# A Fourier mix and a dense block on one core: partial sums of the early dense products put off, and a spare PSUM bank for their refills

## The chip, the cores and the metric

The kernel runs on one core of a Trainium2 chip. A core has a matrix engine (TensorE, PE in the profile, with PEld for its weight loads), a vector engine (VectorE, DVE), a scalar engine (ScalarE, ACT), GpSimd (POOL) and a sync engine (SP) that here only issues loads. Each engine works off its own queue in order; 16 DMA engines move the data that SP and POOL ask for. Matmuls write into PSUM, which this kernel uses as eight banks of 128 x 512 float32; a bank is read and written by VectorE and ScalarE too. The metric is the device time of one execution in microseconds (us), the median of several runs.

## The reference

x has 2048 tokens of width 640. The output mixes a two-dimensional Fourier transform with a dense block, by a gate per token:

```python
g = sigmoid((x * gate_w).sum(-1, keepdims=True))
a = einsum("bsd,ed->bse", x, dft_hid_re); b = einsum("bsd,ed->bse", x, dft_hid_im)
y = einsum("ts,bse->bte", dft_seq_re, a) - einsum("ts,bse->bte", dft_seq_im, b)
h = einsum("bsd,df->bsf", x, w1) + b1          # 640 -> 1728
act = h * tanh(softplus(h))                    # Mish
out = g * y + (1 - g) * einsum("bsf,fd->bsd", act, w2)
```

All is float32. The kernel computes the transposed output, 640 rows by 2048 tokens.

## The kernel before, in words

**Products.** A float32 operand is split in two float32r tiles, a high part (ScalarE, L344 or L335) and a low part (VectorE, L345 or L336), and a product of two blocks takes three matmuls, all at L350 (mm3: high x high, high x low, low x high). Large products are done with Winograd's form of Strassen's scheme: sums and differences of blocks (tt, L314) save an eighth of the block products, and partial products are copied out of PSUM and back into it (copy, L323: f<-ps is a copy out to SBUF, called to_sbuf; ps<-f is a refill of a bank, onto which the next matmuls add).

**Stages.** First, the sequence transform x with cosines and sines, four problems (q = 0 to 3), each with a first, a second and a third part over 8 pairs of row blocks. The first parts of the problems come at the start of the kernel: 1, then 2, 3 and 0. They have only nine matmuls a step (three banks: two in self.a, one in self.d1), and between their steps stand the steps of the early dense products. Then the second and third parts of all four problems (some 118 to 445 us), the hidden transform, the rest of the dense product, and the second dense product with the output.

**Early dense products.** They are the top 768 of the 1728 columns of w1 against the first 1024 tokens (two tiles of 512, t = 0 and 1). The depth of 640 is cut in blocks of 128. early_first does the first two pairs of blocks (depth 256), early_second the next two and the fifth block (depth 384). Each has three units (j = 0 to 2), a generator with 7 or 8 steps; a step is one product of 3 or 6 matmuls. A unit works in two banks, a and b. It multiplies b11 into a, copies a out as p, multiplies t1 into b; multiplies b21 onto a and drains a: that is the output for t = 0; copies p back into a (copy(a, p), the refill), multiplies t2 onto it, drains it as u, and so on. Four outputs of a unit of early_first go to DRAM as early. (They are loaded twice: by early_second, and much later by dense_first, as the part that the rest of the dense product starts from.) In early_second the inner function end loads early, adds it to the bank, applies Mish (L624, out_act) and stores the activation as act. So there a drain of a bank is an add on VectorE that also waits for the load of early.

**Order.** Two lines of three units each run side by side with the running product of the sequence transform: line one is units 0 and 2 of early_first and unit 1 of early_second, line two is unit 1 of early_first and units 0 and 2 of early_second. After each of the 24 steps of problems 2, 3 and 0 stands one step of each line. The running product takes three banks and the two units two each, seven of eight. At a turn from one problem to the next (after 8 and 16 steps) three new banks are taken while three old ones are drained.

**Planner.** The program records all operations with their dependences (Graph.add); Graph.run then plays them on a model of the engines and emits each engine's queue in the order that comes out. PE keeps program order. Another engine takes, when it is free, the ready operation with the earliest due time (want) that is granted its buffers. wants() works the due times out backward from PE's order; `by` makes a due time earlier, `since` bars an operation before a time. A buffer pool (psum, FS for 18 tiles of 128 x 512, and others) grants a buffer if more are free than earlier asks are open (granted); an operation that drains PSUM, or follows such a one, is prompt, and one that is not prompt also leaves buffers for prompt ones that are due within 5 us. If nothing can go on, the planner stops with an error ("stuck"). Loads go through SP's queue (L296), stores through POOL's (L306).

Of the kernel before, what the change touches and what calls it, by code (L numbers as in the profile page):

```python
# [27 lines left out]
DELAY, RATE = 2.2, 370e3  # L28
CALM, CALM_DMA, NEAR = 1.0, 3.0, 3.0
GATES = 130.0, 10.0  # L30
GATED = 600.0, 7.0


# [16 lines left out]
class Graph:  # L50
# [75 lines left out]
    def run(self, pools):  # L126

        self.wants()
        for op in self.ops:
            for v in op.vals:  # L130
                if v.pool and (v.ask is None or op.want < v.ask[0]):
                    v.ask = op.want, op.n, id(v)
        for op in self.ops:
            for v in op.vals:
                if v.pool and v.ask[1] == op.n:
                    also = [u.ask[0] for u in op.vals if u.pool is v.pool and u is not v]
                    if also:
                        v.ask = min(v.ask, (max(also), op.n, id(v)))
        for p in pools:
            p.asks = sorted({v.ask for op in self.ops for v in op.vals if v.pool is p})  # L140
            p.soon = sorted({v.ask for op in self.ops if op.prompt for v in op.vals if v.pool is p and v.ask[1] == op.n})
        missing = {op.n: len(op.deps) for op in self.ops}
        free = {e: 0.0 for e in ("PE", "ACT", "DVE", "SP", "POOL")}
        ready = {e: [] for e in free}
        pe = [op.n for op in self.ops if op.engine == "PE"][::-1]
        for op in self.ops:
            if not missing[op.n]:
                insort(ready[op.engine], (op.want, op.n))
        events, now, left, dma = [], 0.0, len(self.ops), 0.0
        waits = sorted({op.since for op in self.ops})  # L150

        def granted(op, blocked):
            for v in op.vals:
                if v.pool and v.t is None:
                    if v.pool in blocked:
                        return False
                    p, n = v.pool, bisect_left(v.pool.asks, v.ask)
                    if not op.prompt:
                        n += bisect_left(p.soon, (v.ask[0] + AHEAD,)) - bisect_left(p.soon, v.ask)
                    if len(p.free) <= n:  # L160
                        blocked.add(v.pool)
                        return False
            return True

        def bequeath(p):
            if p.heir and not p.asks:
                p.heir.free += [p.part(t) for t in p.free]
                p.free = []

        while left:  # L170
            began = False
            for e, line in ready.items():
                if free[e] > now + 1e-9 or not line:
                    continue
                if e == "PE":
                    i = next((i for i, x in enumerate(line) if x[1] == pe[-1]), None)
                    if i is not None and not granted(self.ops[pe[-1]], set()):
                        i = None
                else:
                    blocked = set()  # L180
                    i = next((i for i, x in enumerate(line)
                              if self.ops[x[1]].since <= now and granted(self.ops[x[1]], blocked)), None)
                if i is None:
                    continue
                op = self.ops[line.pop(i)[1]]
                if e == "PE":
                    pe.pop()
                for v in op.vals:
                    if v.pool and v.t is None:
                        v.pool.asks.remove(v.ask)  # L190
                        if v.ask in v.pool.soon:
                            v.pool.soon.remove(v.ask)
                        v.t = v.pool.free.pop(0)
                        bequeath(v.pool)
                op.emit()
                free[e] = now + op.hold
                if e in ("SP", "POOL"):
                    dma = max(now + DELAY, dma) + op.moves
                    end = dma + 0.1
                else:  # L200
                    end = now + op.took + 0.03
                heapq.heappush(events, (end, op.n, False))
                left -= 1
                began = True
            if began:
                continue
            times = [t for e, t in free.items() if t > now + 1e-9 and ready[e]]
            times += [t for t in waits if t > now][:1]
            if events:
                times.append(events[0][0])  # L210
            assert times, ("stuck", left, pe and self.ops[pe[-1]].at, [(p.name, len(p.free)) for p in pools])
            now = max(now, min(times))
            while events and events[0][0] <= now + 1e-9:
                _, n, held = heapq.heappop(events)
                op = self.ops[n]
                if held:
                    insort(ready[op.engine], (op.want, op.n))
                    continue
                for v in op.vals:
                    v.left -= 1  # L220
                    if not v.left and v.pool:
                        p = v.pool
                        p.free.append(v.t)
                        bequeath(p)
                for a in op.after:
                    missing[a.n] -= 1
                    if not missing[a.n]:
                        wait = min(CALM_DMA if op.engine in ("SP", "POOL") else CALM, a.want - now - NEAR)
                        if a.engine in ("ACT", "DVE") and wait > 0:
                            heapq.heappush(events, (now + wait, a.n, True))  # L230
                        else:
                            insort(ready[a.engine], (a.want, a.n))
# [8 lines left out]
def fnet_mish_gate(ctx: ExitStack, tc: tile.TileContext, xn, xt, c_re, c_im, wd_re, wd_im,  # L241
# [56 lines left out]
        op.by, op.since = by, since  # L298
        return v

    def load_of(pool, d, rows=P):
        return load(pool, lambda: d.t, d, rows)

    def store(d, v, rows=P, queue=None):
        queue = queue or STORES
# [313 lines left out]
    def raw(t, k):  # L619
        return load(FS, xt[t, k])  # L620
# [80 lines left out]
        out_act(FC, t, a, a, FR, False)  # L701

    H = FP // 2
    early = {(t, f): dram(f"early{t}_{f}") for t in range(2) for f in range(FP)}

    def w1_twice(k0, fifth=False):

# [37 lines left out]
    def early_first():  # L745
# [3 lines left out]
        def unit(j):  # L749
            a, b = bank(), bank()  # L750
            mm3(a, at["b11", j], x["a11"], True, True)
            p = to_sbuf(a)
            yield
            mm3(b, at["t1", j], x["s1"], True, True)
            yield
            mm3(a, at["b21", j], x["a12"], False, True)
            store(early[0, j], to_sbuf(a))
            copy(a, p)
            yield
            mm3(a, at["t2", j], x["s2"], False, True)  # L760
            u = to_sbuf(a)
            yield
            mm3(a, at["t3", j], x["s3"], False, True)
            v = to_sbuf(a)
            tt(v, b, v, OP.add)
            store(early[1, j + H], v)
            yield
            mm3(b, at["b22", j], x["s4"], False, True)
            tt(u, b, u, OP.add)
            store(early[0, j + H], u)  # L770
            yield
            mm3(a, at["t4", j], x["a22"], False, True)
            store(early[1, j], to_sbuf(a))
            yield
        return [unit(j) for j in range(H)]

    def early_second():
# [4 lines left out]
        def unit(j):  # L782
            a, b = bank(), bank()

            def end(c, t, f):
                o = load_of(FS, early[t, f])
                tt(o, c, o, OP.add)
                out_act(f, t, o, o)
            mm3(a, at["b11", j], x["a11"], True, True)
            p = to_sbuf(a)  # L790
            yield
# [1 line left out]
            yield  # L793
            mm3(a, at["b21", j], x["a12"], False, False)
            mm3(a, at[("d", 0), j], d[0], False, True)
            end(a, 0, j)
            copy(a, p)
            yield
            mm3(a, at["t2", j], x["s2"], False, True)
            u = to_sbuf(a)  # L800
# [9 lines left out]
            yield  # L810
            mm3(a, at["t4", j], x["a22"], False, False)
            mm3(a, at[("d", 0), j], d[1], False, True)
            end(a, 1, j)
            yield
            copy(b, v)
            mm3(b, at[("d", 1), j], d[1], False, True)
            end(b, 1, j + H)
            yield
        kept.update(x, d=d)
        return [unit(j) for j in range(H)]  # L820
# [3 lines left out]
    def early_rests():  # L824
        for t, ks in ((0, ("a11", "a12")), (1, ("a21", "a22"))):
            dense_rest(t, [operand(raw(t, k)) for k in range(2)] + [kept[k] for k in ks] + [kept["d"][t]])

    def dense_first(tp):
        t1, t2 = tp, tp + 2
# [145 lines left out]
    ua, ub = early_first(), early_second()  # L975
    lines = [ua[0], ua[2], ub[1]], [ua[1], ub[0], ub[2]]
    lines = [(u for q in line for u in q) for line in lines]
    for q in (2, 3, 0):
        for _ in sq[q].steps(seq_top):
            for line in lines:  # L980
                next(line, None)
    for line in lines:
        for _ in line:
            pass
# [1 line left out]
    for q in range(4):  # L986
        sq[q].second(seq.low)
        if q == 2:
            gates()
        sq[q].third()  # L990
    hd[0].first(hid.top)
    hd[1].first(hid.top)
    for p in hd:
# [58 lines left out]
```

## Time and profile before

| | |
|---|---|
| median of 3 runs | 865.77 us (864.66 to 866.73) |
| profiled execution, device time | 866.31 us |
| its span, first to last instruction | 864.5 us |
| TensorE busy | 856.1 us (99%), 3754 matmuls |
| VectorE, ScalarE, GpSimd busy | 694.5, 486.9, 91.8 us |
| DMA | 220.27 MB, mean 255 GB/s |
| mean granted TensorE clock | 0.998 |

A row of the timeline reads: start in us, duration, engine, line, operation, output<-inputs by the program's tile names, shapes, count, and in brackets the idle time of the engine before it and what ended it. Matmul durations overlap: matmuls are pipelined, and the time of one is the distance of two starts. A row of waits reads: who waited for whom, us in total, times, longest. A row of windows reads: the stretch, its length, busy time and instructions of PE, PEld, DVE, ACT and POOL, then the granted clock (1.00 is full speed), the mean busy share of the DMA engines, and GB/s. A row of the chain of work that ended last reads: start, us, what.

### The profile page before, as it was taken

To read this page: it belongs to the slowest core of one execution; us is meant where nothing else is said; L and a number is where in the kernel's file an instruction comes from. 1 tells how busy PE (TensorE), PEld (TensorE's weight loads), DVE (VectorE), ACT (ScalarE), POOL (GpSimd) and SP (SyncE) were. 2 spreads that over 40 slices of the span, in tenths; PEclk is the share of its full clock that TensorE was granted. 3 is DMA by queue.
4 is the path that set the end of the run, shared out by engine and by line. 5 is a ranking of instruction groups with operands and counts; after the bars stand their busy time and mean duration, and the time that the engine had idled before them with its cause. 6 is when DMAs were issued, how large, how long until landed. Compare 5 with 4: busy or idle time off the path is not lost.

```text
span 864.5 us, 12193 instructions
## 1 busy us (share of the span) xinstructions
PE 856.1 (99%) x3754; PEld 704.8 (82%) x3754; DVE 694.5 (80%) x1241; ACT 486.9 (56%) x902; POOL 91.8 (11%) x167
## 2 busy tenths in 40 slices
PE   8999999999999999999999999999999999999998
PEld 6887788888888888888888888888888888888886
DVE  7978789986896778677999978997787996758493
ACT  6976776535354654456576733676566764533242
POOL 0122110002000200100020001022222100004000
PEclk9999999999999999999999999999999999999999
DMA  9888786777885957395778839678798876637943
GB/s 331 303 321 303 258 284 235 258 250 268 306 278 177 357 178 233 129 346 194 233 239 314 298 111 368 228 249 304 272 306 314 314 257 239 197 117 170 367 163 122
DMA packets 110946, 220.27 MB, mean 255 GB/s; under 512 B 13920, under 2 KB 18144, under 8 KB 110880
## 3 DMA queue, kind: packets, MB, share of 16 engines
q1 hardware_dynamic: 97184, 177.14, 60.0%
q0 software_dynamic: 13552, 42.22, 13.9%
q8 instruction: 29, 0.48, 0.2%
q14 instruction: 37, 0.30, 0.1%
q10 hardware_dynamic: 144, 0.13, 0.0%
HBM read 174.59 MB, written 44.84 MB: 254 GB/s over the span
## 4 chain that ended last, share of the span: by engine, by line
PE 97%; DMA 2%; DVE 0%; ACT 0%; issue 0%; SPq 0%; ACTq 0%; DVEq 0%
PE ps L350 97%; DMA x<-in_xn_dram 1%; DMA x<-in_w1a_dram 1%; DMA f<-in_c_im_dram 1%; SPq L296 0%; DVE f L314 0%; DVE x L314 0%; DVE r1l L345 0%; DVE r4l L345 0%; ACT r1h L344 0%; ACT ps L323 0%; ACT w19h L335 0%; ACT f L323 0%; DVE f L601 0%; ACT f L599 0%
## 5 line engine op out<-in xcount | busy, mean ns | idle before, releaser
L314 DVE TENSOR_TENSOR f<-f,f 128x512 f32<-128x512 f32 (+1 forms) x322 | 214.2, 683 | 5.1 <-DMA f<-act 2.0
L323 ACT ACTIVATE f<-ps 128x512 f32<-128x512 f32 x149 | 87.1, 595 | 63.4 <-PE ps L350 58.0
L314 DVE TENSOR_TENSOR f<-ps,f 128x512 f32<-128x512 f32 x101 | 66.9, 685 | 44.2 <-PE ps L350 34.2
L306 POOL DMA_DIRECT2D u<-f x40 | 21.6, 541 | 303.2 <-DVE f L314 289.8
L344 ACT ACTIVATE r9h<-f 128x512 fp32r<-128x512 f32 x40 | 25.3, 631 | 29.0 <-PE ps L350 20.5
L306 POOL DMA_DIRECT2D act<-f x52 | 28.1, 541 | 116.8 <-ACT f L624 74.1
L344 ACT ACTIVATE r5h<-f 128x512 fp32r<-128x512 f32 x38 | 24.0, 631 | 28.0 <-PE ps L350 22.2
L314 DVE TENSOR_TENSOR x<-x,x 128x256 f32<-128x256 f32 (+2 forms) x88 | 38.0, 445 | 2.2 <-DMA x<-in_xn_dram 1.5
L344 ACT ACTIVATE r1h<-f 128x512 fp32r<-128x512 f32 x39 | 24.5, 629 | 25.1 <-PE ps L350 19.6
L344 ACT ACTIVATE r4h<-f 128x512 fp32r<-128x512 f32 x38 | 23.9, 630 | 24.3 <-PE ps L350 18.7
L323 ACT ACTIVATE ps<-f 128x512 f32<-128x512 f32 x56 | 33.0, 598 | 8.2 <-DVE f L314 7.8
L344 ACT ACTIVATE r0h<-f 128x512 fp32r<-128x512 f32 x38 | 23.9, 629 | 23.8 <-PE ps L350 14.2
L344 ACT ACTIVATE r6h<-f 128x512 fp32r<-128x512 f32 x38 | 24.0, 631 | 23.2 <-PE ps L350 14.6
L344 ACT ACTIVATE r2h<-f 128x512 fp32r<-128x512 f32 x38 | 23.9, 629 | 22.8 <-PE ps L350 16.6
L344 ACT ACTIVATE r7h<-f 128x512 fp32r<-128x512 f32 x38 | 24.0, 631 | 21.5 <-PE ps L350 11.9
L345 DVE TENSOR_TENSOR r9l<-f,r9h 128x512 fp32r<-128x512 f32 x40 | 27.5, 686 | 10.5 <-ACT r9h L344 10.3
L344 ACT ACTIVATE r3h<-f 128x512 fp32r<-128x512 f32 x39 | 24.5, 628 | 19.9 <-PE ps L350 14.0
L344 ACT ACTIVATE r8h<-f 128x512 fp32r<-128x512 f32 x36 | 22.7, 630 | 21.2 <-PE ps L350 10.9
L345 DVE TENSOR_TENSOR r6l<-f,r6h 128x512 fp32r<-128x512 f32 x38 | 26.1, 686 | 10.4 <-ACT r6h L344 10.2
L345 DVE TENSOR_TENSOR r1l<-f,r1h 128x512 fp32r<-128x512 f32 x39 | 26.7, 686 | 9.0 <-ACT r1h L344 8.6
L624 ACT ACTIVATE f<-f,b1s 128x512 f32<-128x512 f32 x36 | 25.9, 718 | 14.1 <-DVE f L314 13.8
L345 DVE TENSOR_TENSOR r2l<-f,r2h 128x512 fp32r<-128x512 f32 x38 | 26.1, 688 | 9.5 <-ACT r2h L344 8.9
(2185 smaller groups left out, 2696.2 us busy)
## 6 DMA issues: line engine op xcount, KB each, us to landing
f<-in_c_im_dram SPq DMA_DIRECT2D x128, 256.0 KB, 4.7
f<-in_c_re_dram SPq DMA_DIRECT2D x128, 256.0 KB, 4.2
f<-act SPq DMA_DIRECT2D x84, 256.0 KB, 4.6
f<-u SPq DMA_DIRECT2D x80, 256.0 KB, 4.1
act<-f POOLq DMA_DIRECT2D x52, 256.0 KB, 4.0
f<-in_xt_dram SPq DMA_DIRECT2D x42, 256.0 KB, 4.3
u<-f POOLq DMA_DIRECT2D x40, 256.0 KB, 4.2
x<-in_xn_dram SPq DMA_DIRECT2D x24, 320.0 KB, 4.8
```

The costliest lines, as they stand in the source:

```text
L306: dma(queue, lambda: ISSUE[queue].dma_start(d.t, v.t[:rows]), whole(v), whole(d), rows * N * 4)
L314: dve(lambda: nc.vector.tensor_tensor(o.t[rows, x], a.t[rows, y], b.t[rows, z], op=op), whole(a, b), whole(o), n)
L323: act(lambda: nc.scalar.activation(o.t, a.t, AF.Copy, scale=scale), whole(a), whole(o))
L344: act(lambda: nc.scalar.activation(r.t[0][:, :N], src.t[:, :N], AF.Copy), whole(src), [(r, 0)])
L345: dve(lambda: nc.vector.tensor_tensor(r.t[1][:, :N], src.t[:, :N], f32(r.t[0][:, :N]), op=OP.subtract), whole(src) + [(r, 0)], [(r, 1)])
L350: G.add("PE", lambda: nc.tensor.matmul(bank.t, w.t[wn][:, k * P:k * P + P], x.t[xn_][:, :N], start, stop, skip_group_check=True), [(w, (k, ...
L624: act(lambda: nc.scalar.activation(o.t[rows], src.t[rows], AF.Mish, **more), whole(src, table) + whole(b1s) * bias, whole(o), more=0.1)
```

## The change

Four things change:

- early_second no longer adds early. Its function end stores its output tile in DRAM as late; banks a (twice) and b (once) of a unit are drained for it by to_sbuf.
- A new function early_acts, after the third parts of the sequence problems in program order, loads early and late for each of the 12 outputs, adds them in SBUF, applies Mish and stores act. Its loads carry since = 300 + 8 i us (SUMS), its adds are due 8 us later.
- The refill of p goes into a newly taken bank (a = copy(bank(), p)) in place of the bank that was just drained, in both kinds of units. A unit so holds three banks for a while; the eighth is used. copy(b, v) at the end of a unit of early_second stays as it is.
- The second line begins one step behind the first: after the first of the 24 steps only the first line steps. And the planner, where nothing at all can go on, tries once more with a flag (tight) by which a prompt operation counts only prompt asks ahead of it.

```diff
+SUMS = 300.0, 8.0
...
+                    if op.prompt and tight:
+                        n = bisect_left(p.soon, v.ask)
...
+            if not times and not tight:
+                tight = True
+                continue
             assert times, ("stuck", left, pe and self.ops[pe[-1]].at, [(p.name, len(p.free)) for p in pools])
...
-    def load_of(pool, d, rows=P):
-        return load(pool, lambda: d.t, d, rows)
+    def load_of(pool, d, rows=P, since=0.0):
+        return load(pool, lambda: d.t, d, rows, since=since)
...
-    early = {(t, f): dram(f"early{t}_{f}") for t in range(2) for f in range(FP)}
+    early, late = ({(t, f): dram(f"{n}{t}_{f}") for t in range(2) for f in range(FP)} for n in ("early", "late"))
...
             store(early[0, j], to_sbuf(a))
-            copy(a, p)
+            a = copy(bank(), p)
...
-            def end(c, t, f):
-                o = load_of(FS, early[t, f])
-                tt(o, c, o, OP.add)
-                out_act(f, t, o, o)
+            def end(o, t, f):
+                store(late[t, f], o)
...
-            end(a, 0, j)
-            copy(a, p)
+            end(to_sbuf(a), 0, j)
+            a = copy(bank(), p)
...
-            end(a, 1, j)
+            end(to_sbuf(a), 1, j)
             yield
             copy(b, v)
             mm3(b, at[("d", 1), j], d[1], False, True)
-            end(b, 1, j + H)
+            end(to_sbuf(b), 1, j + H)
...
+    def early_acts():
+
+        for i, key in enumerate(early):
+            since = SUMS[0] + SUMS[1] * i
+            o, v = (load_of(FS, d[key], since=since) for d in (early, late))
+            tt(o, o, v, OP.add)
+            G.ops[-1].by = since + SUMS[1]
+            out_act(key[1], key[0], o, o)
...
-    for q in (2, 3, 0):
-        for _ in sq[q].steps(seq_top):
-            for line in lines:
-                next(line, None)
+    for n, _ in enumerate(s for q in (2, 3, 0) for s in sq[q].steps(seq_top)):
+        for line in lines if n else lines[:1]:
+            next(line, None)
...
+    early_acts()
     hd[0].first(hid.top)
```

More of the change, by code (lines that the diff above doesn't have):

```diff
@@ L168, in bequeath @@
                 p.free = []
+        tight = False
         while left:
@@ L205, in run @@
             if began:
+                tight = False
                 continue
```

## The prediction

> **What bounds the kernel now.** I read the page's busy shares first, then what TensorE waited for over the whole run, then the chain of work that ended last, and from there the timelines of the two places where the chain leaves TensorE.
>
> ```profile
> PE 856.1 (99%) x3754; PEld 704.8 (82%) x3754; DVE 694.5 (80%) x1241; ACT 486.9 (56%) x902; POOL 91.8 (11%) x167
> ```
>
> ```profile
> PE ps L350 <- ACT ps L323: 2.4, 2, 1.9
> ```
>
> ```profile
> 7.94 68.75 PE ps L350 x302
> ...
> 92.33 0.59 ACT ps L323
> ...
> 92.96 767.73 PE ps L350 x3377
> ```
>
> TensorE (PE) is the bound, and the diff adds and removes no matmul. So only time in which PE stands still or runs slow can be won. After the start-up there are two such waits in the whole run, both for ScalarE (ACT) writing a PSUM bank (L323, output ps), and the chain leaves PE between 77 and 93 us only. From 92.96 us to 860.69 the chain is PE alone. The next rows are PE's, around both waits and behind them.
>
> ```profile
> 85.12 0.39 PE L350 MATMUL ps<-r0h,w1l 128*128 128x512 f32 x1
> 86.03 0.50 PE L350 MATMUL ps<-r6h,w25h 128*128 128x512 f32 x1 [0.52 <-ACT ps L323]
> ...
> 87.53 0.40 PE L350 MATMUL ps<-w24h,w21h 128*128 128x512 f32 x1
> ...
> 90.72 0.39 PE L350 MATMUL ps<-r1h,w25l 128*128 128x512 f32 x1
> 92.96 0.50 PE L350 MATMUL ps<-r6h,w25h 128*128 128x512 f32 x1 [1.85 <-ACT ps L323]
> ...
> 97.42 0.39 PE L350 MATMUL ps<-r5h,w22h 128*128 128x512 f32 x1
> ...
> 103.78 0.39 PE L350 MATMUL ps<-w24l,w9h 128*128 128x512 f32 x1
> ```
>
> ```profile
> 92.00:94.00 2.00, 1.04 (x4) 0.85 (x5) 1.87 (x4) 2.00 (x4) 0.15 (x1) 0.93 0.80 309
> 94.00:96.00 2.00, 2.00 (x7) 1.52 (x6) 1.93 (x5) 1.15 (x3) 0.39 (x1) 0.50 0.93 346
> ```
>
> At full speed matmuls start (103.78 - 97.42) / 28 = 0.227 us apart. The first wait costs 86.03 - 85.12 - 0.23 = 0.68 us, and the six matmuls behind it 1.50 - 6 x 0.227 = 0.14. The second costs 92.96 - 90.72 - 0.23 = 2.01, and the twelve matmuls from 92.96 to 97.42 take 4.46 where 12 x 0.227 = 2.72 would do: 1.74 more, because the granted clock (the seventh figure of the window rows) fell to 0.50 right behind the wait. Together 4.57 us, 0.53% of the run: the most that the change can win here.
>
> **Why the two refills were late.** Both are the line copy(a, p) of a unit of early_second: bank a, drained after the third product, gets the first product back, and the fourth product adds to it. The ACT and DVE (VectorE) rows before them:
>
> ```profile
> 83.11 0.42 DVE L314 TENSOR_TENSOR x<-x,x 128x256 f32<-128x256 f32 x1 [1.48 <-DMA x<-in_xn_dram]
> ...
> 84.66 0.68 DVE L314 TENSOR_TENSOR f<-ps,f 128x512 f32<-128x512 f32 x1
> ...
> 89.38 0.68 DVE L314 TENSOR_TENSOR f<-ps,f 128x512 f32<-128x512 f32 x1
> ```
>
> ```profile
> 79.20 0.58 ACT L323 ACTIVATE f<-ps 128x512 f32<-128x512 f32 x1
> ...
> 82.01 0.58 ACT L323 ACTIVATE f<-ps 128x512 f32<-128x512 f32 x1
> ...
> 85.38 0.60 ACT L323 ACTIVATE ps<-f 128x512 f32<-128x512 f32 x1 [2.08 <-DVE f L314]
> ...
> 90.84 0.63 ACT L344 ACTIVATE r0h<-f 128x512 fp32r<-128x512 f32 x1 [1.48 <-DMA f<-in_xt_dram]
> 91.68 0.74 ACT L335 ACTIVATE w19h<-x 128x640 fp32r<-128x640 f32 x1 [0.21 <-DMA x<-in_w1a_dram]
> 92.33 0.58 ACT L323 ACTIVATE ps<-f 128x512 f32<-128x512 f32 x1
> ```
>
> First refill: the drain (the add at 84.66) stood on DVE behind an op that waited 1.48 us for a load of xn; the refill followed it at once. Second: the drain ended at 90.06, but in ACT's queue the refill stood behind two conversions that waited for loads, and began 2.27 us later. In both, drain and refill have to fit into the one stretch of other matmuls between two products of a unit.
>
> **The change, part by part.** *The refill into a new bank* depends only on the first product's copy p, not on the drain. For the second of the two waits p was written by the copy at 82.01 (79.20 is a drain of the running product), and the refill was wanted at 90.95 (90.72 + 0.23): a refill that may start from 82.6 on has some 8 us, where it had 90.95 - 90.06 = 0.9 from the end of the drain. It needs a free bank: three of the running product and two of each unit make 7 of 8. The offset of one step lets the first unit's drained bank serve the second. I take both waits and their tails as gone: -4.57. Its bounds are 0 (the refill keeps its place in ACT's order) and -4.57.
>
> *Drains of the second half.* Per unit four loads of early, four adds and four Mish leave this stage, and three ACT copies from PSUM come in (the fourth sum is drained by the add into u, as before).
>
> ```profile
> L323 ACT ACTIVATE f<-ps 128x512 f32<-128x512 f32 x149 | 87.1, 595 | 63.4 <-PE ps L350 58.0
> L314 DVE TENSOR_TENSOR f<-ps,f 128x512 f32<-128x512 f32 x101 | 66.9, 685 | 44.2 <-PE ps L350 34.2
> L306 POOL DMA_DIRECT2D act<-f x52 | 28.1, 541 | 116.8 <-ACT f L624 74.1
> ...
> L624 ACT ACTIVATE f<-f,b1s 128x512 f32<-128x512 f32 x36 | 25.9, 718 | 14.1 <-DVE f L314 13.8
> ```
>
> ```profile
> 48.00:76.00 28.00, 28.00 (x125) 23.21 (x124) 23.45 (x48) 22.64 (x46) 5.65 (x11) 1.00 0.92 328
> 76.00:112.00 36.00, 33.63 (x140) 26.97 (x140) 26.58 (x52) 24.47 (x47) 5.94 (x11) 0.95 0.80 274
> 300.00:400.00 100.00, 100.00 (x443) 82.80 (x442) 74.08 (x117) 46.35 (x78) 5.37 (x10) 1.00 0.63 217
> ```
>
> For three units: DVE -12 x 0.685 = -8.2 us, ACT -12 x 0.718 + 9 x 0.595 = -3.3 us, SP and the DMA engines -12 loads of 256 KB = 3.1 MB, about 10 us of what 48 to 76 us moves (328 GB/s); POOL issues 12 stores of late in place of 12 of act, 0.54 us each as before. All of it lies beside PE, so it is worth 0 by itself; it thins the queues that made the refills late, since an op behind a late load on ACT or DVE holds whatever stands behind it. A drain now waits only for PE and its place in ACT's queue, not for a load of early.
>
> *early_acts, from 300 us on.* 24 loads, 12 adds of 0.685 us (8.2 us of DVE), 12 Mish (8.6 us of ACT), 12 stores on POOL (6.5 us of issue). In the window DVE has 26 us idle, ACT 54, POOL 95. DMA: 36 x 0.262 = 9.4 MB in the 96 us that SUMS spreads them over, 98 GB/s on top of 217, under the 328 that 48 to 76 us carried. What hides it is the lead of the operands:
>
> ```profile
> 293.91 0.69 DVE L345 TENSOR_TENSOR r7l<-f,r7h 128x512 fp32r<-128x512 f32 x1 [0.67 <-ACT r7h L344]
> ```
>
> ```profile
> 304.15 0.39 PE L350 MATMUL ps<-r7l,w21h 128*128 128x512 f32 x1
> ```
>
> This is the shortest lead that I find between 300 and 400 us: written by 294.60, used at 304.15, 9.5 us. The densest stretch there is the turn near 370 to 385 us (GB/s in 40 slices of 2.5 us from 300 on):
>
> ```profile
> GB/s 371 234 256 270 173 105 7 247 68 230 189 295 234 218 265 331 225 145 182 108 105 87 18 158 55 187 308 334 404 398 395 400 392 381 222 50 0 20 316 311
> ```
>
> In those 20 us near 400 GB/s, 98 more make a delay of 20 x 98 / 400, some 5 us at most, under the lead. Queued behind an early_acts load on SP are c tiles; behind the add on DVE low parts of operands; both have that lead. I take 0; bounds 0 and +3.75, one wait with its slow tail like the second one above.
>
> *Second line one step behind.* PE's first step with units loses 3 matmuls to a later place, so the next steps come 0.68 us sooner. The nearest operand there:
>
> ```profile
> 27.99 0.28 DVE L336 TENSOR_TENSOR w10l<-x,w10h 128x128 fp32r<-128x128 f32 x1
> ```
>
> ```profile
> 28.68 0.39 PE L350 MATMUL ps<-r0h,w10l 128*128 128x512 f32 x1
> ```
>
> w10l is there at 28.27 and would be asked for at 28.00: a new wait of 0.3 us, or none where DVE takes it sooner; bounds 0 and 0.68. I take 0.3, the value that the two rows give. The last step of the second line now falls into the last of the 24 steps, so nothing hangs over.
>
> Sum: -4.57 + 0.3 = -4.3. The profiled execution took 866.31 us with a span of 864.5, which would give 862.0; the median of the runs lies 0.54 under it, so 865.77 - 4.3 = 861.5. What is late next in this stage is copy(b, v), which refills the same bank as before:
>
> ```profile
> 105.66 0.60 ACT L323 ACTIVATE ps<-f 128x512 f32<-128x512 f32 x1 [0.46 <-DVE f L314]
> ```
>
> ```profile
> 106.95 0.39 PE L350 MATMUL ps<-w23h,w22h 128*128 128x512 f32 x1
> ```
>
> It had 106.95 - 106.26 = 0.7 us to spare.
>
> **A page's rule against the trace.** The granted clock halved behind a wait of 1.85 us and stayed whole behind 0.52 us. The Trainium skill, TensorE: Matmul & The Clock Gate, section "What's actually happening", has the clock drop after an idle window of about 3.4 us. Taken at its word the 1.85 us wait was too short to be the cause, and the slow stretch would come back without it. The trace sets the two side by side, so I follow the trace.
>
> **Rivals.** (1) *The wait moves* (the change doesn't do what it says): ACT's order is written by the planner, which wants a refill just ahead of its use, so a refill, or copy(b, v) with its 0.7 us, can still stand behind a conversion that waits 1.5 us for a load. For: 90.84 above. Against: refills that are ready early go when ACT is free, and fewer loads are due. One wait of 2.01 + 1.74 is left: 861.5 + 3.75 = 865.2.
>
> (2) *Slower: banks run out at the turns.* At its turns (8 and 16 steps in) the running product needs three new banks while its old three are being drained. Before, the eighth was spare; now a refill may hold it, and the products of the next problem wait for ACT's drains. Such a drain already waited behind a load at one turn:
>
> ```profile
> 78.83 0.47 ACT L662 ACTIVATE w14h<-x 128x320 fp32r<-128x320 f32 x1 [0.79 <-DMA x<-in_w1b_dram]
> ```
>
> The third drain followed at 79.20. Against: the planner gives banks in the order of need, and the running product needs them sooner than the refill. At two turns with 2.01 + 1.74 each: 861.5 + 7.5 = 869.0. It decides from new waits of 4.3 + 1.7 = 6.0 us on.
>
> (3) *The slow clock stays without the wait*: 861.5 + 1.74 = 863.2.
>
> **How the numbers follow.** Forecast 0.60, rival 1 0.13, rival 2 0.22, rival 3 0.05. A change of 0.2% (1.7 us) is about what a measurement of this kernel can tell from none. Under 864.0 lie the forecast, rival 3 and 0.02 of rival 1: faster 0.67; within, 0.09 of rival 1 and 0.01 of rival 2: 0.10; slower, the rest, 0.23. The forecast's own range is 860.5 (both waits gone and no new one, 861.2, less 0.7, a third of the 2.07 us from the fastest to the slowest of the three runs) to 863.5; with 0.60 + 0.05 + 0.13 it is not yet 8 in 10, so the range reaches to rival 2's time: 860.5 to 869.0.
>
> **What would show it.** Right: PE's waits for ACT ps are gone between 77 and 100 us, the clock reads 1.00 there, refills start several us ahead of their matmuls, loads of early stand between 300 and 400 us with no PE wait there. Wrong: a PE wait above 1 us for a bank at a turn (near 48 or 78 us), or for operands anywhere, with a clock under 1.00 behind it.

## The result, and the profile after

The changed kernel takes 861.79 us, the median of 6 runs (861.36 to 862.17); on the same chip the kernel before takes 865.25 (863.77 to 866.73). The ratio is 0.9959, with a 95% interval of 0.9946 to 0.9972: 0.41% faster. The forecast was 861.5. Of the 51 executions of the kernel before that the experiments were compared with, 23 had a mean granted clock of 0.998 or less and took 865.93 to 868.22 us, and 28 had 0.999 or 1.000 and took 863.85 to 866.23; the profiled one, from which the prediction took its price, has 0.998.

The page after, the busy shares:

```profile
PE 854.1 (99%) x3754; PEld 704.4 (82%) x3754; DVE 692.7 (81%) x1241; ACT 491.6 (57%) x911; POOL 98.3 (11%) x179
```

As many matmuls and VectorE instructions as before, nine ScalarE instructions more (the drains) and twelve POOL issues more (the stores of late). The chain of work that ended last (start, us, what), from the start-up to the end:

```profile
2.12 4.92 DMA f<-in_c_im_dram
...
7.06 0.64 ACT r1h L352
...
7.72 0.70 DVE r1l L353
...
8.47 847.89 PE ps L358 x3739
```

Behind the start-up the chain is one unbroken piece of PE (L358 is L350 of before), where there were two with 16 us of other engines between them. From the first long piece's start to the last matmul's end it was 860.69 - 7.94 = 852.75 us before, and is 856.36 - 8.47 = 847.89 now: 4.86 us less, of which this execution gives 8.47 - 7.94 = 0.53 back at the start, where a load of c_im took 4.92 us and not 4.39. What TensorE waited for over the whole run, all rows:

```profile
PE ps L358 <- ACT r1h L352: 1.0, 1, 1.0
PE ps L920 <- PEq L1055: 0.8, 1, 0.8
PE ps L358 <- DVE r1l L353: 0.2, 1, 0.2
PE ps L358 <- DVE r0h L350: 0.2, 1, 0.2
```

All four stand in the start-up. The row for ACT ps is gone. The windows (length, busy time of PE, PEld, DVE, ACT, POOL, granted clock, DMA share, GB/s), same stretches as before:

```profile
48.00:76.00 28.00, 28.00 (x125) 23.18 (x125) 22.07 (x46) 20.19 (x41) 5.90 (x11) 1.00 0.90 324
76.00:112.00 36.00, 36.00 (x161) 29.81 (x160) 25.38 (x49) 26.86 (x53) 7.01 (x13) 1.00 0.64 222
...
300.00:400.00 100.00, 100.00 (x443) 82.84 (x442) 74.60 (x120) 53.66 (x92) 11.84 (x22) 1.00 0.84 293
```

Between 76 and 112 us PE is busy throughout, at the full clock, and the DMA engines move 222 GB/s where it was 274; from 300 to 400 us they move 293 where it was 217, and PE loses nothing.

So the time went where the prediction said. Whether it went for the reason that it gave is what the experiments ask. To sum the time that PE lost in a stretch, I add up by how much each distance of two matmul starts exceeds 0.227 us (where it does by more than 0.01). For 48 to 118 us that gives 4.6 us before and 0.0 after.

### The profile page after: what moved, and what is told of

Same layout as the page of the kernel before. It is cut to its first block, busy times and chain, and to the rows that moved or that the text cites. A ratio compares the mean times of both kernels' runs of the same rounds, so it can differ in the third digit from the quotient of the medians.

```text
span 860.4 us, 12262 instructions
## 1 busy us (share of the span) xinstructions
PE 854.1 (99%) x3754; PEld 704.4 (82%) x3754; DVE 692.7 (81%) x1241; ACT 491.6 (57%) x911; POOL 98.3 (11%) x179
## 4 chain that ended last, share of the span: by engine, by line
PE 99%; DMA 1%; SPq 0%; DVE 0%; ACT 0%; issue 0%; ACTq 0%
PE ps L358 99%; DMA f<-in_c_im_dram 1%; SPq L304 0%; DVE r1l L353 0%; ACT r1h L352 0%; DVE f L609 0%; ACT f L607 0%; ACTq L607 0%
## 5 line engine op out<-in xcount | busy, mean ns | idle before, releaser
L322 DVE TENSOR_TENSOR f<-f,f 128x512 f32<-128x512 f32 x331 | 220.5, 687 | 5.6 <-DMA f<-act 1.7
L331 ACT ACTIVATE f<-ps 128x512 f32<-128x512 f32 x158 | 93.0, 596 | 69.0 <-PE ps L358 62.4
L322 DVE TENSOR_TENSOR f<-ps,f 128x512 f32<-128x512 f32 x92 | 60.9, 687 | 42.3 <-PE ps L358 29.1
L314 POOL DMA_DIRECT2D act<-f x52 | 28.1, 541 | 174.6 <-ACT f L632 131.8
L314 POOL DMA_DIRECT2D u<-f x40 | 21.5, 541 | 206.8 <-DVE f L322 194.8
L352 ACT ACTIVATE r8h<-f 128x512 fp32r<-128x512 f32 x39 | 24.6, 629 | 24.2 <-PE ps L358 14.7
L353 DVE TENSOR_TENSOR r0l<-f,r0h 128x512 fp32r<-128x512 f32 x41 | 28.2, 689 | 10.9 <-ACT r0h L352 10.7
L352 ACT ACTIVATE r2h<-f 128x512 fp32r<-128x512 f32 x39 | 24.5, 628 | 19.0 <-PE ps L358 14.3
L352 ACT ACTIVATE r7h<-f 128x512 fp32r<-128x512 f32 x36 | 22.7, 630 | 21.4 <-PE ps L358 11.9
L353 DVE TENSOR_TENSOR r8l<-f,r8h 128x512 fp32r<-128x512 f32 x39 | 26.9, 688 | 9.6 <-ACT r8h L352 9.4
L352 ACT ACTIVATE r1h<-f 128x512 fp32r<-128x512 f32 x39 | 24.5, 627 | 16.0 <-PE ps L358 12.2
```

Of the source, the lines that this page charges most:

```text
L314: dma(queue, lambda: ISSUE[queue].dma_start(d.t, v.t[:rows]), whole(v), whole(d), rows * N * 4)
L322: dve(lambda: nc.vector.tensor_tensor(o.t[rows, x], a.t[rows, y], b.t[rows, z], op=op), whole(a, b), whole(o), n)
L331: act(lambda: nc.scalar.activation(o.t, a.t, AF.Copy, scale=scale), whole(a), whole(o))
L352: act(lambda: nc.scalar.activation(r.t[0][:, :N], src.t[:, :N], AF.Copy), whole(src), [(r, 0)])
L353: dve(lambda: nc.vector.tensor_tensor(r.t[1][:, :N], src.t[:, :N], f32(r.t[0][:, :N]), op=OP.subtract), whole(src) + [(r, 0)], [(r, 1)])
```

## Experiments

Three theories stood at the start. A: the refill that no longer follows the drain wins. B: the early stage with less to load and to do wins. C: the waits were an accident of one order of the queues. Each run is compared with the kernel before on the same chip; where I compare two variants, I do so by their ratios.

**The refill and the offset without the sums put off.**

```diff
-            def end(o, t, f):
-                store(late[t, f], o)
+            def end(c, t, f):
+                o = load_of(FS, early[t, f])
+                tt(o, c, o, OP.add)
+                out_act(f, t, o, o)
...
-            end(to_sbuf(a), 0, j)
+            end(a, 0, j)
             a = copy(bank(), p)
...
-    early_acts()
```

> The changed kernel with the early sums undone: early_second loads early and adds it out of the bank on VectorE as before, Mish at once, no early_acts; the refill into a new bank and the offset of the lines stay. Theory A (the refill that no longer follows the drain is what wins): no TensorE wait for a bank between 24 and 118 us, clock 1.00 throughout, 861.8 us within 0.7. Theory B (the thinner queues win): the refills are not what was late, one or two waits as before stay, 864 to 865.3. Theory C (the two waits were an accident of one order of the queues, and any other order is free of them): 861.8 as well.

864.62 us, ratio 0.9986 (0.9975 to 0.9996). PE lost 2.8 us between 48 and 118 us in the profiled execution. All that PE waited for after 20 us:

```profile
PE ps L358 <- DVE f L322: 1.5, 1, 1.5
PE ps L358 <- ACT f L331: 0.7, 1, 0.7
```

The waits for a refill of p are gone, as theory A has it, but two others took their place, both for drains. The longer one, with VectorE's rows ahead of it:

```profile
101.00 0.69 DVE L322 TENSOR_TENSOR f<-f,f 128x512 f32<-128x512 f32 x1
101.60 0.69 DVE L322 TENSOR_TENSOR f<-ps,f 128x512 f32<-128x512 f32 x1
102.20 0.68 DVE L353 TENSOR_TENSOR r0l<-f,r0h 128x512 fp32r<-128x512 f32 x1
102.80 1.28 DVE L322 TENSOR_TENSOR f<-ps,f 128x512 f32<-128x512 f32 x2
```

```profile
103.54 0.50 PE L358 MATMUL ps<-r6h,w22h 128*128 128x512 f32 x1 [1.48 <-DVE f L322]
```

VectorE works without a pause, three drains (f<-ps,f) and other operations in turn, and PE waits for a bank that a drain has yet to free. Theory A falls as an account of the whole gain.

**The sums put off without the new bank.** Both refills are copy(a, p) again, into the bank just drained; the offset stays.

```diff
-            a = copy(bank(), p)
+            copy(a, p)
```

> The changed kernel with the refill undone: copy(a, p) into the bank that was just drained, in both kinds of units; the sums put off and the offset stay. Theory A: drain and refill again stand in one stretch between two products, some 1 us to spare, so at least one wait for a refill of 0.5 us or more between 24 and 118 us: 862.5 to 865.3. Theory B: no wait, 861.8. Theory C: 861.8.

861.73 us, ratio 0.9948 (0.9928 to 0.9968): the whole gain. PE lost 0.0 us between 48 and 118 us, though the refills are as tight as theory A feared: the tightest pair that I find in ScalarE's and TensorE's rows is

```profile
36.90 0.60 ACT L331 ACTIVATE ps<-f 128x512 f32<-128x512 f32 x1
```

```profile
37.73 0.39 PE L358 MATMUL ps<-r3h,w13h 128*128 128x512 f32 x1
```

that is 37.73 - 37.50 = 0.23 us. Here such a narrow lead cost nothing.

**Without the offset, and the offset alone.**

```diff
-        for line in lines if n else lines[:1]:
+        for line in lines:
```

> The changed kernel with both lines stepping from the first step on. Theory A: in the first two pairs of units the first line's refill takes the eighth bank, and the second line's has to wait for a drain, so its lead over its matmul falls to 1 us or so, where it was several; a wait only if a load holds ScalarE: 861.8 to 863. If the offset is needed for the gain: waits of 1 us or more at the second line's fourth product, 863 to 865.3. Theories B and C: 861.8.

861.71 us, ratio 0.9948 (0.9928 to 0.9968). The offset is not needed.

The other way round, the kernel before with the offset alone:

```diff
-    for q in (2, 3, 0):
-        for _ in sq[q].steps(seq_top):
-            for line in lines:
-                next(line, None)
+    for n, _ in enumerate(s for q in (2, 3, 0) for s in sq[q].steps(seq_top)):
+        for line in lines if n else lines[:1]:
+            next(line, None)
```

> The kernel before with nothing but the second line one step behind. Theories A and B: refills and queues are as before, waits for a bank of 0.5 to 2 us stay near 85 to 95 us or move by a step: 863.5 to 866. Theory C: the order of all queues is new, so the waits are gone: 861.8.

864.58 us, ratio 0.9984 (0.9974 to 0.9995), with one PE wait of 1.2 us for a drain on VectorE. A new order of the queues moves the waits and shortens them, but does not free the stage of them: theory C explains 0.16%, not the rest.

**The sums put off alone.** The kernel before with neither new bank nor offset, only late and early_acts; against the changed kernel:

```diff
-            a = copy(bank(), p)
+            copy(a, p)
...
-        for line in lines if n else lines[:1]:
+        for line in lines:
```

> The kernel before with the sums put off alone: refill into the drained bank, both lines in step. If putting off is the whole gain: no wait of TensorE between 24 and 118 us, 861.7. If the offset is needed where the refill is not: a wait of 0.5 us or more at the turns (near 48 or 78 us), where the products of both lines and the next problem ask for banks at once: 862.5 to 865.

861.98 us, ratio 0.9958 (0.9944 to 0.9972). No PE wait after the start-up, 0.0 us lost between 48 and 118 us. One of the change's parts is the whole gain, and it is the one that I had priced at 0.

**What of it: the drain that waits for a load, the work, or the traffic?** First the drain apart from the load: ScalarE copies the bank, VectorE adds early to the copy when early is there. All the stage's loads, adds, Mish and stores are back, and early_acts is gone (refill into the drained bank, offset).

```diff
-            def end(o, t, f):
-                store(late[t, f], o)
+            def end(v, t, f):
+                o = load_of(FS, early[t, f])
+                tt(o, v, o, OP.add)
+                out_act(f, t, o, o)
```

> late_only with the sums back in the early stage, but the drain apart from the load: ScalarE copies the bank to SBUF, VectorE adds early to that copy when it has landed, Mish and store at once; refill into the drained bank, offset kept. The stage has all its loads, adds, Mish and stores of before, and nine copies more. Theory B1 (less traffic and work in the stage is what wins): waits stay, 864 to 865.5. Theory B2 (a drain that waits for no load of early and does not stand in VectorE's queue is what wins): no wait, 861.8.

863.72 us, ratio 0.9976 (0.9966 to 0.9986): between the two theories; PE lost 2.0 us from 48 to 118 us. The offset is in this run, and alone it gave 0.9984 (0.9974 to 0.9995). The two intervals overlap, so it is not shown that the drain apart wins anything by itself. Nor do the adds of the kernel before stand waiting for early: the profile's list of who waited for this tile has one row, ScalarE's with 0.3 us, and none of VectorE.

The same with the refill into a new bank, so that neither these drains nor the refill hang on a load:

```diff
-            copy(a, p)
+            a = copy(bank(), p)
```

> drain_apart with the refill into a new bank: everything that early_second did in the early stage is still there (loads of early, adds, Mish, stores), but neither a drain nor a refill of p waits for a load or for VectorE. If the late drain and the late refill are all that PE waited for (theory B2 and A together): no wait, 861.8. If the stage is simply too full (theory B1): waits for a bank stay, as with drain_apart, 863 to 864.5.

863.69 us, ratio 0.9977 (0.9967 to 0.9988), 1.9 us lost. On top of drains that are apart, the new bank adds nothing. The longest wait that is left, 0.87 us, is again for a drain on VectorE. The chain that leads to it goes through a store (its row names a bank, but it is issued at L314, the line of the stores), the drain on ScalarE that follows when the store has landed, and a load:

```profile
77.78 7.12 DMA ps<-f
...
84.98 0.60 ACT f L331
...
95.41 3.95 DMA f<-in_c_re_dram
```

What the store and the drain have in common is a buffer of the pool FS, which the one reads and the other writes; so these buffers can be what is short, as well as the DMA engines.

What is missing of the gain lies in the stage's load, so I put its two parts back one at a time. The engines' work, to the kernel with the sums put off and nothing else but the offset (the added results are used by nothing; the output is as before):

```diff
             def end(o, t, f):
                 store(late[t, f], o)
+                v = fresh(FS, o, o, OP.add)
+                mish(v, v, f)
```

> late_only with the engines' work put back and no traffic: at each of the 12 drains VectorE adds the drained tile to itself and ScalarE applies Mish to that sum, which nothing uses; the output is as before. If VectorE and ScalarE are the thick queues (B1 by work): waits of 0.5 us or more between 75 and 105 us, 862.5 to 865. If work is not it: no wait, 861.8.

861.97 us, ratio 0.9959 (0.9944 to 0.9974), 0.2 us lost. The work is in the stage (from 76 to 112 us ScalarE is busy for 31.4 us, before the change for 24.5), and twelve adds and twelve Mish there cost nothing that can be measured. It is not the work. This run and the one with the drains apart and the new bank were timed on one chip: 861.74 to 862.25 over four executions here, 862.43 to 864.11 over ten there. Besides the new bank, which costs the changed kernel nothing, what the other has in the stage and this one has not is the 12 loads of early, with the adds that need them. By the two ratios that is worth 0.18%.

Then the traffic, first as 12 loads of early into buffers of the pool, which nothing uses:

```diff
             def end(o, t, f):
                 store(late[t, f], o)
+                load(FS, lambda: early[t, f].t, early[t, f], by=G.pe)
```

> late_only with 12 loads of early put back into the early stage, due when they were before; nothing uses what they load. Theory B1: the DMA engines and SP's queue are as full as before, loads of operands come late again, ScalarE or VectorE stand behind them: a wait of 0.5 us or more between 75 and 105 us, 862.5 to 865.3. Theory B2: no wait, 861.8.

873.28 us, ratio 1.0088 (1.0065 to 1.0111): slower than before. But this run is not clean. A drain of ScalarE reused the buffer of such a load and had to wait for its landing:

```profile
62.01 1.08 ACT L331 ACTIVATE f<-ps 128x512 f32<-128x512 f32 x2 [1.91 <-DMA f<-early]
```

So I put the traffic in without any buffer, as copies from DRAM to DRAM:

```diff
             def end(o, t, f):
                 store(late[t, f], o)
+                c = dram(f"copied{t}_{f}")
+                dma("SP", lambda: nc.sync.dma_start(c.t, early[t, f].t), whole(early[t, f]), whole(c), P * N * 4)
+                G.ops[-1].by = G.pe
```

> late_only with the traffic of the 12 loads of early put back without any buffer: 12 copies of 256 KB from early to other DRAM, issued by SP and due when the loads were. Nothing waits for them. If the DMA engines are the thick queue (B1 by traffic): loads of operands land later, a wait of 0.5 us or more between 60 and 105 us, 862.5 to 866. If traffic is not it: no wait, 861.8.

874.34 us, ratio 1.0100 (1.0079 to 1.0122). PE's waits, all rows above 0.5 us after the start-up:

```profile
PE ps L358 <- ACT f L331: 2.7, 2, 1.5
PE ps L358 <- ACT ps L331: 2.5, 1, 2.5
PE ps L358 <- ACT w13h L343: 1.4, 1, 1.4
...
PE ps L358 <- DVE w13l L344: 0.6, 1, 0.6
```

The waits for banks are back, for drains and for a refill, and ahead of the first of them ScalarE stands still because a store has not landed:

```profile
59.75 0.60 ACT L331 ACTIVATE f<-ps 128x512 f32<-128x512 f32 x1 [2.19 <-DMA ps<-f]
```

With the copies PE loses 7.7 us between 48 and 118 us, more than before the change. But this run does not show that transfers alone do it either. A copy reads early, so in SP's queue it stands until the store of that tile has landed, and the loads behind it stand with it. SP's waits at the copies from 48 to 112 us:

```profile
SPq L796 <- DMA early<-f: 15.0, 5, 4.3
```

Before the change all loads together waited 4.3 us there for stores of early:

```profile
SPq L296 <- DMA early<-f: 4.3, 2, 2.6
```

Nor was the stage fuller: from 40 to 118 us the DMA engines moved 20.5 MB here, 21.1 MB without the copies and 22.7 MB before the change. And PE also lost 6.1 us before 24 us (1.6 before the change), at the rows for w13, though the first copy is issued at 41.88 us: there only the order has changed, because the planner works out due times backward through one shared row of DMA work. So neither run puts the traffic back and nothing else. That the loads cost by their traffic stays unproven.

**early_acts, closer together.**

```diff
-SUMS = 300.0, 8.0
+SUMS = 300.0, 1.0
```

> The changed kernel with the twelve sums 1 us apart from 300 us on, not 8. If the lead of the operands (7 to 10 us there) is what hides early_acts: 24 loads are 6.3 MB, some 16 us of the DMA engines at 400 GB/s ahead of the c tiles, more than the lead, so one or two waits of TensorE for operands of 2 to 6 us between 300 and 330 us and a slow clock behind them: 864 to 870. If the planner fits them in behind the c tiles, or the buffers limit them: 861.8.

866.42 us, ratio 1.0006 (0.9996 to 1.0015): the gain is gone. PE loses 4.8 us between 300 and 400 us, all in waits for operands between 322 and 334 us; the longest rows:

```profile
329.54 0.50 PE L358 MATMUL ps<-r7h,w12h 128*128 128x512 f32 x1 [0.85 <-ACT r7h L352]
...
333.88 0.50 PE L358 MATMUL ps<-r3l,w11h 128*128 128x512 f32 x1 [0.65 <-DVE r3l L353]
```

```profile
300.00:340.00 40.00, 37.19 (x157) 28.80 (x156) 26.85 (x44) 22.28 (x37) 6.48 (x12) 1.00 0.92 330
```

24 loads within 12 us use up the lead of the operands. Spaced by 8 us they cost nothing.

**Waits of known length, for the clock.** 16 waits were put into the sequence transform; the values stay the same.

```diff
+    def mm3(bank, b, x, start, stop, hold=0):
         w, k = b
         mm(bank, w, k, 0, x, 0, start, False)
         mm(bank, w, k, 0, x, 1, False, False)
+        for _ in range(hold):
+            copy(bank, bank)
...
+    HOLD = {(sq[q], part, k): (2, 3, 4, 6)[(q + 2 * (part == 3) + (k == 4)) % 4]
+            for q in range(4) for part in (2, 3) for k in (1, 4)}
```

> The changed kernel with 16 waits of TensorE put into the second and third parts of the sequence transform, each 13 us or more from the next: ahead of the third matmul of a product ScalarE copies the bank onto itself 2, 3, 4 or 6 times (four places each; the values stay the same). With 0.6 us a copy and 0.3 for the hand-over: waits of 1.5, 2.1, 2.7 and 3.9 us, together 41 us. If a wait like the one of 1.85 us halves the clock (rival 3 falls): a stretch at 0.50 behind most waits of 2.1 us and more, 1.7 us each: some 861.8 + 41 + 20 = 923. By the rule that only an idle window of about 3.4 us does it: behind the four longest alone, 861.8 + 41 + 7 = 910.

928.89 us in one run. TensorE's rows of four of the waits, and the windows of 14 us around those four:

```profile
145.90 0.50 PE L358 MATMUL ps<-r9h,w15l 128*128 128x512 f32 x1 [1.98 <-ACT ps L331]
167.83 0.50 PE L358 MATMUL ps<-r1h,w13l 128*128 128x512 f32 x1 [2.59 <-ACT ps L331]
290.45 0.50 PE L358 MATMUL ps<-r1h,w9l 128*128 128x512 f32 x1 [1.37 <-ACT ps L331]
460.93 0.50 PE L358 MATMUL ps<-r6h,w13l 128*128 128x512 f32 x1 [1.98 <-ACT ps L331]
```

```profile
143.00:157.00 14.00, 12.02 (x54) 9.62 (x53) 13.07 (x25) 7.14 (x13) 0.00 (x0) 1.00 0.74 264
164.00:178.00 14.00, 11.41 (x44) 8.89 (x43) 11.92 (x21) 5.39 (x9) 0.00 (x0) 0.88 0.70 224
288.00:302.00 14.00, 12.63 (x56) 10.14 (x55) 5.55 (x9) 5.49 (x9) 0.00 (x0) 1.00 0.29 91
458.00:472.00 14.00, 12.02 (x47) 9.41 (x46) 12.68 (x25) 7.92 (x15) 0.00 (x0) 0.88 0.71 214
```

All 16, by idle time of PE in the row and clock of the 14 us window around it:

| idle before the matmul, us | waits | with a slow stretch (0.88 in the window) |
|---|---|---|
| 1.37 | 3 | 0 |
| 1.88, 1.98, 1.99 | 3 | 0 |
| 1.98, 2.03 | 2 | 2 |
| 2.59, 2.64, 3.12, 3.36, 3.82, 3.87, 4.32, 4.38 | 8 | 8 |

Every slow window has the same mean of 0.88: (1 - 0.88) x 14 / 0.5 = 3.4 us at half clock, whatever the wait. The 30 matmuls behind such a wait took 1.45 to 1.77 us too long, behind the others 0.13 to 0.17. At about 2 us of idle it falls either way.

## Why the prediction was right, and where it was not

*The bound and the price of the waits* were right. The prediction read 4.57 us off PE's distances; by the same sum over 48 to 118 us 4.6 were lost before and 0.0 after, and the chain's PE piece is 4.86 us shorter. That the forecast of 861.5 lies only 0.3 us from the measured 861.79 is partly luck. In the new comparison the runs of before have a median of 865.25, not 865.77, and against that the change won 3.46 us where 4.3 were forecast. The price was read off one execution with a slow stretch, whose tail is 1.74 us of the 4.57. One such stretch, 3.4 us at half clock, takes 0.002 off the mean clock of 865 us, and by the clocks given with the result fewer than half of the executions have one. Also, this execution of the changed kernel gives 0.53 us back at the start. By the ratio the gain is 0.41% where 0.49% was forecast, inside the interval.

*The step "The refill into a new bank ... I take both waits and their tails as gone: -4.57"* named the wrong part. With the offset it brings 0.14%, no more than the offset alone (0.16%), and its waits pass on to drains; without it the gain is whole (0.9948), and beside drains that are apart from loads it adds nothing. The prediction quoted two rows as causes, a VectorE operation that waits 1.48 us for xn and a ScalarE conversion that waits 1.48 us for xt. The runs bear these rows out: from 48 to 112 us the waits of ScalarE and VectorE for loads, added up, are 5.8 us before, 2.4 to 8.3 us in the four variants that keep the loads of early where they were (the refill with the offset, the offset alone, and the two with the drains apart), and 0.6 to 1.6 us in the changed kernel and the variants without those loads (no new bank, the sums put off alone, the work put back). The question to ask was which part of the change ends those waits, not which part lets the refill step around them.

*The step "it is worth 0 by itself; it thins the queues"* is the one that failed: putting the sums off, alone, is worth 0.42%. How this divides is known in part. The work that leaves is worth nothing, and the loads that leave are worth 0.18%, by the run with the work put back against the one with the drains apart and the new bank. The rest is not separated: the best variant with the loads still there, at 0.9976, holds the offset, which alone is worth 0.16%. The prediction's remark that a drain now waits for no load of early has no row behind it: the trace of the kernel before shows no drain on VectorE that waited for one. With the loads of early gone, not every load lands sooner: those of xn and xt, the loads in the two rows quoted above, do, and those of c_re land later. The list of DMA issues from 48 to 112 us (count, KB each, median us to landing), before and after:

```profile
f<-in_c_re_dram SPq DMA_DIRECT2D x21, 256.0 KB, 4.6
...
x<-in_xn_dram SPq DMA_DIRECT2D x5, 320.0 KB, 6.2
...
f<-in_xt_dram SPq DMA_DIRECT2D x5, 256.0 KB, 5.0
```

```profile
f<-in_c_re_dram SPq DMA_DIRECT2D x21, 256.0 KB, 5.2
...
x<-in_xn_dram SPq DMA_DIRECT2D x7, 320.0 KB, 5.0
...
f<-in_xt_dram SPq DMA_DIRECT2D x4, 256.0 KB, 3.9
```

*early_acts at 0* was right, with its reason: the lead of the operands. The shortest lead of an operand tile r between 300 and 400 us fell from 9.5 to 4.2 us (366.56 to 370.81, by the rows below), a loss of 5.3 us, about the 5 us of delay that the prediction allowed for a burst (one weight tile there had 1.7 us left), and with the sums 1 us apart it ran out.

```profile
365.87 0.69 DVE L353 TENSOR_TENSOR r2l<-f,r2h 128x512 fp32r<-128x512 f32 x1 [1.99 <-ACT r2h L352]
```

```profile
370.81 0.39 PE L358 MATMUL ps<-r2l,w12h 128*128 128x512 f32 x1
```

*The 0.3 us for w10l* did not come: PE waits for nothing there, the lower of the two bounds. The tiles have other numbers in the changed kernel, so the rows don't show whether VectorE took that operand sooner.

*Rival 1* (the wait moves) did not happen to the whole change, but it is what happens to its refill alone: one of the two waits there, 0.7 us, came about behind copy(b, v). *Rival 2*: no wait at either turn; how near it was, was not tried. *Rival 3* falls: the clock stayed at 1.00 with the waits gone, and the deliberate waits bring slow stretches back. The rule of the Trainium skill that the prediction weighed (TensorE: Matmul & The Clock Gate, section "What's actually happening"), by which the clock drops after an idle window of about 3.4 us, asks for too long an idle time: 1.98 us was enough in one of two such waits, and each one of 2.59 us or more did it. The same section of the Trainium skill has the full clock come back after about 3.4 us of sustained work, and the slow stretch measured here has that length, 3.4 us.

The flag tight plays no part: the planner never comes to the point where it would be set, in the changed kernel.

What stays open is by what the loads of early cost: their time on the DMA engines, their places in SP's queue, the buffers of the pool FS that they hold, or the order that the planner writes when more loads are due. Putting transfers back changed several of these at once.

## What to carry to other kernels

When an engine's in-order queue makes the bound engine wait, find out which load it stands behind and ask what could leave that stage, before giving the waiter another buffer: here, putting the sums off, which takes 3 MB of loads out of the full stage at the price of 6.3 MB more traffic in all, was the whole gain, and the spare bank added nothing to it. Price "thinner queues" not at zero but at the waits whose rows end in a DMA. Space out what is moved, too: the same work within 12 us cost all that it had won. When a transfer is put back as a test, look at what it waits for: a copy that stands in a queue for its own source tests the queue as well as the traffic.

## What the runs showed of the hardware

The clock's slow stretch has one length, 3.4 us, whatever the wait was, and costs 1.45 to 1.77 us; in the one execution with deliberate waits, those of 1.37 us never brought one (3 of 3 without), those of 1.88 to 2.03 us did in two of five, longer ones always (8 of 8). So a wait that grows from 1.9 to 2.6 us can cost 0.7 + 1.7 = 2.4 us and not 0.7, an estimate from these rows. Kernels whose waits were gone also scattered less: 861.36 to 862.17 over six runs, where before it was 863.77 to 866.73.
